# Output rows leaving in transfers of two tiles from four buffers, in a Fourier-mixing and gated feed-forward kernel

## The chip, the cores and the metric

The kernel runs on one core of a Trainium2 chip. A core has a TensorE for matrix products (PE in the profile, its weight loads PEld), a VectorE (DVE), a ScalarE (ACT), a GpSimd (POOL) and a SyncE (SP), which here only issues transfers; 16 DMA engines carry the transfers. The metric is the device time of one execution in microseconds (us), lower is better. The kernel before takes 1181.79 us in the median of three runs (1179.18, 1181.79 and 1183.06).

## The reference

The input `x` has 8 batches of 3136 rows of 256 numbers. First it is transformed by a Fourier transform over the rows and over the columns, of which the real part is kept. Then comes a gated feed-forward block:

```python
X = np.fft.fft(np.fft.fft(x, axis=1), axis=2).real          # (8, 3136, 256)
h = np.maximum(X @ w_in, 0.0)                               # (8, 3136, 1024)
conv = sum(conv_w[k] * shifted(h, k - 1) for k in range(3)) # three taps along the rows, zeros at the ends
out = (h * sigmoid(conv)) @ w_out                           # (8, 3136, 256), float32
```

`shifted(h, j)` stands for `h` moved by `j` rows.

## The kernel before

The sequence transform is done once per batch as matrix products with tables (`pd`, the `Unit`s in the code), spread over the steps of the batch before. Its results lie in `PQ`. The rest is a loop of 256 steps: 8 batches, 4 chunks of a batch, and 8 blocks of 128 columns out of the 1024 of the middle layer (`steps`, line 925). A step `(b, c, f)` goes through several engines in a software pipeline written out by hand (lines 1019 to 1052; nothing is reordered by a planner):

- `products` (line 777): two matmuls into the PSUM tiles `pb` and `pa`; `copies` (784), ScalarE, copies `pb` to `nb`; `combine` (792), VectorE, makes `h` of both, which applies the relu.
- `first_tap` (801), ScalarE, starts the tile `g` with the first tap; `middle` (806) adds the second tap by an accumulating transfer `g<-h`, which GpSimd issues; `last_tap` (810), VectorE, three steps later, adds the third.
- `sigmoid` (824), ScalarE, and `gate` (830), GpSimd and VectorE, four steps later.
- `mm2` (846), five steps later (`LAG`): TensorE multiplies each tile of 128 rows of `g` with its block of `wout` and sums over the eight blocks `f` in the PSUM tiles `po`, two row tiles in each.

The output path is the end of `mm2`. A chunk has six row tiles. The last chunk of a batch has 64 rows more; they are kept in `left`, and in an odd batch the rows left of two batches make a seventh tile. At the eighth block, when a pair of tiles in `po` is complete, ScalarE copies both to a buffer `os` in SBUF (line 861), and SP issues one transfer of 128 KB for each tile (line 863), or two of 64 KB for the seventh tile. There are three buffers `os` (line 80); a copy into a buffer waits until the transfers out of it have landed. So every eight steps there is a burst of six copies and six transfers, and at the end of the batches 1, 3, 5 and 7 one of seven copies and eight transfers.

Each engine runs its instructions strictly in the written order. Behind the copies of a burst ScalarE has the sigmoid, the copies of `pb` and of the transform's tiles (`as<-pd`, lines 381 and 405) of the next steps. SP's queue also holds the loads of `x` (`xh`, lines 119 and 126) and of a row that is spread over the partitions (`eb`, line 562).

A row of ones, `one` (line 665), lies in the pool of constants. Two matmuls before the loop read it (line 915). The pool `gp` (line 78) has seven slots that hold set-up tiles first and then the tiles `g` in turn.

Of the kernel before, what the change touches and what calls it, by code (L numbers as in the profile page):

```python
# [9 lines left out]
F32 = mybir.dt.float32  # L10
# [27 lines left out]
def kernel(  # L38
# [10 lines left out]
    nc = tc.nc  # L49
    B, S, D = x.shape  # L50
    F = moe_w_in.shape[1]
    P = 128
# [16 lines left out]
    const = ctx.enter_context(tc.tile_pool(name="const", bufs=1))  # L69
# [7 lines left out]
    hp = ctx.enter_context(tc.tile_pool(name="hp", bufs=6))  # L77
    gp = ctx.enter_context(tc.tile_pool(name="gp", bufs=7))
    nbp = ctx.enter_context(tc.tile_pool(name="nbp", bufs=2))
    osp = ctx.enter_context(tc.tile_pool(name="osp", bufs=3))  # L80
    edp = ctx.enter_context(tc.tile_pool(name="edp", bufs=1, space=DRAM))
    psa = ctx.enter_context(tc.tile_pool(name="psa", bufs=2, space=PSUM))
    psb = ctx.enter_context(tc.tile_pool(name="psb", bufs=1, space=PSUM))
# [8 lines left out]
    def mm(o, l, r, start, stop):  # L92
        nc.tensor.matmul(o, l, r, start=start, stop=stop, skip_group_check=True)  # L93
# [568 lines left out]
            for f in self.parts(c0, c1):  # L662
                f()

    one = const.tile([1, P], F32, name="one")
    nc.gpsimd.memset(one, 1.0)
    ident = gp.tile([3 * NF, 3 * NF], F32, name="ident", tag="g")
    make_identity(nc, ident)
# [87 lines left out]
    rows = out.rearrange("b s d -> (b s) d")  # L756
# [89 lines left out]
    def mm2(s):  # L846
        b, c, f = s
        ch = chunks[c]
        tiles = [(gs[s][:, o:o + m], [(0, b, r, m)]) for o, r, m in ch.tiles]
        if ch.last and b % 2:  # L850
            tiles.append((left[:, f], [(i * LEFT, b - 1 + i, ch.rest[1], LEFT) for i in range(2)]))
        for i, (w, to) in enumerate(tiles):
            if f == 0 and i % 2 == 0:
                po[b, c, i // 2] = pso.tile([P, 2, D], F32, name="po", tag="po")
            pt = po[b, c, i // 2]
            mm(pt[:, i % 2, :], w, wout[:, f, :], f == 0 and i % 2 == 0, f == NF - 1)
            if f == NF - 1 and (i % 2 or i == len(tiles) - 1):
                del po[b, c, i // 2]
                osb = osp.tile([P, 2, D], F32, name="os", tag="os")
                for j in range(i - i % 2, i + 1):  # L860
                    nc.scalar.copy(out=osb[:, j % 2], in_=pt[:, j % 2])  # L861
                    for p0, b_, r, m in tiles[j][1]:
                        nc.sync.dma_start(out=rows[b_ * S + r:b_ * S + r + m, :], in_=osb[p0:p0 + m, j % 2])
        gs.pop(s)


# [152 lines left out]
    for t in range(n + LAG):  # L1019
# [30 lines left out]
        if t >= LAG:  # L1050
            mm2(steps[t - LAG])
# [67 lines left out]
```

## Time and profile before

The profiled execution took 1182.34 us; its span, from the first instruction to the last, is 1180.6 us, and the mean granted TensorE clock 0.995.

| | us | share of the span |
|---|---|---|
| TensorE, matmuls | 1142.3 | 97% |
| TensorE, weight loads (beside the matmuls) | 889.1 | 75% |
| VectorE | 970.7 | 82% |
| ScalarE | 943.5 | 80% |
| GpSimd | 611.2 | 52% |
| copies `os<-po` on ScalarE, 196 of them | 57.8 | 5% |

The transfers `g<-h` are the largest traffic (115.83 MB on their queue); the queue of SP and ScalarE moves 50.89 MB, of which 25.7 MB are written to HBM.

In the profile a row of the timeline gives a start, a length, the engine, the line, the operation, what is written and read, and in brackets how long the engine stood idle before and who ended that. The chain of waits is the work that ended last, followed back from the end of the program. In the name of an engine a `q` means its sequencer, which waits and issues transfers. The granted clock is the share of TensorE's full clock that it was given in a stretch.

### The profile page before, as it was taken

How to read it: one execution, taken by the hardware profiler on the slowest of the kernel's cores; microseconds unless marked ns; L12 is line 12 of the kernel's file. 1: busy time of each engine (PE TensorE's matmuls, PEld its weight loads, DVE VectorE, ACT ScalarE, POOL GpSimd, SP SyncE). 2: the span in 40 equal slices, each digit the busy share in tenths (PEclk: the TensorE clock that was granted, in tenths of full speed). 3: DMA queues.
4: the chain of work that ended last, by engine and by line, in shares of the span. 5: the costliest groups of instructions: out<-in, count | busy, mean ns of one | idle time of the engine just before them, and what ended most of it. 6: DMA issues, size and time to landing. Idle time of an engine off the chain costs nothing.

```text
span 1180.6 us, 16071 instructions
## 1 busy us (share of the span) xinstructions
PE 1142.3 (97%) x4818; PEld 889.1 (75%) x4818; DVE 970.7 (82%) x1448; ACT 943.5 (80%) x1939; POOL 611.2 (52%) x734
## 2 busy tenths in 40 slices
PE   4989999999999999999998999999999999999998
PEld 2756777777777777777776777777778777777777
DVE  7589979998788789798876888888787678788885
ACT  2578878888788879888876878888887788898884
POOL 5346745666366554746464464655444344444443
PEclk9999999999999999999999999999999999999999
DMA  8767886776677676757675576865565556666664
GB/s 209 196 101 156 167 142 155 163 162 141 142 157 164 131 180 133 170 113 175 144 168 120 107 156 139 181 128 121 128 124 107 124 122 138 129 131 127 128 117 99
DMA packets 107587, 168.16 MB, mean 142 GB/s; under 512 B 32657, under 2 KB 62627, under 8 KB 107501
## 3 DMA queue, kind: packets, MB, share of 16 engines
q0 software_dynamic: 41984, 115.83, 51.3%
q1 hardware_dynamic: 64345, 50.89, 15.3%
q8 instruction: 38, 0.62, 0.2%
q10 hardware_dynamic: 1172, 0.43, 0.2%
q14 instruction: 48, 0.39, 0.1%
HBM read 38.40 MB, written 25.74 MB: 54 GB/s over the span
## 4 chain that ended last, share of the span: by engine, by line
PE 77%; ACT 5%; DVE 3%; issue 1%; DMA 1%; POOL 0%; ACTq 0%; DVEq 0%; SPq 0%
PE po L93 48%; PE pb L93 12%; PE pa L93 11%; PE pd L93 6%; ACT nb L790 1%; ACT g L828 1%; DVE g L813 1%; ACT os L861 1%; DMA out_dram<-os 1%; ACT pa L769 0%; ACT g L804 0%; DVE g L837 0%; DVE h L798 0%; DVE w L228 0%; DVE pt L418 0%
## 5 line engine op out<-in xcount | busy, mean ns | idle before, releaser
L93 PE MATMUL po<-wout,g 128*128 128x256 f32 x3072 | 709.3, 380 | 6.9 <-DVE g L837 6.2
L93 PEld LDWEIGHTS po<-wout,g 128*128 128x128 f32 x3072 | 582.7, 190 | 152.9 <-issue 20.0
L808 POOL DMA_DIRECT2D g<-h x256 | 228.3, 892 | 460.9 <-ACT g L804 247.4
L828 ACT ACTIVATE g<-g,cw 128x385 f32<-128x385 f32 (+2 forms) x512 | 291.9, 624 | 67.3 <-DVE g L813 64.8
L836 POOL TENSOR_TENSOR g<-g,h 128x385 f32<-128x385 f32 (+1 forms) x256 | 305.6, 1194 | 55.9 <-ACT g L828 54.2
L790 ACT ACTIVATE nb<-pb 128x386 f32<-128x386 f32 (+3 forms) x512 | 227.0, 498 | 113.0 <-PE pb L93 112.2
L798 DVE CUSTOM_DVE_ANT_0 h<-pa,nb 128x386 f32<-128x386 f32 (+3 forms) x512 | 264.5, 557 | 29.8 <-POOL h L775 19.8
L813 DVE SCALAR_TENSOR_TENSOR g<-h,cw,g 128x770 f32<-128x770 f32 (+1 forms) x256 | 284.1, 1110 | 0.0
L804 ACT ACTIVATE g<-h,cw 128x770 f32<-128x770 f32 (+1 forms) x256 | 244.2, 954 | 0.0
L93 PE MATMUL pb<-qt,G 127*128 127x387 f32 (+2 forms) x512 | 214.7, 500 | 2.6 <-ACT nb L790 1.1
L93 PE MATMUL pa<-pt,G 128*128 128x387 f32 (+2 forms) x512 | 213.0, 497 | 1.2 <-ACT pa L769 0.8
L837 DVE TENSOR_TENSOR g<-g,h 128x385 f32<-128x385 f32 (+1 forms) x256 | 187.3, 732 | 25.7 <-ACT g L828 25.5
L769 ACT ACTIVATE pa<-eb,ge 128x387 f32<-128x387 f32 (+2 forms) x256 | 155.1, 606 | 1.4 <-DVE h L798 1.0
L93 PEld LDWEIGHTS pa<-pt,G 128*128 128x128 f32 x512 | 96.7, 190 | 76.8 <-issue 17.3
L93 PE MATMUL pd<-tab,w 98*128 98x197 f32 (+2 forms) x448 | 98.4, 319 | 4.6 <-DVE as L412 3.8
L132 POOL DMA_INDIRECT xh<-in_x_dram,idx x64 | 91.0, 1422 | 18.3 <-issue 12.3
L93 PEld LDWEIGHTS pb<-qt,G 127*128 127x128 f32 x512 | 91.0, 191 | 9.8 <-ACT nb L790 2.9
L93 PEld LDWEIGHTS pd<-tab,w 98*128 98x128 f32 (+1 forms) x448 | 81.8, 191 | 15.0 <-ACT pa L769 5.0
L861 ACT COPY os<-po 128x256 f32<-128x256 f32 x196 | 57.8, 393 | 13.1 <-PE po L93 6.5
L168 DVE TENSOR_TENSOR xh<-xh 98x1024 f32<-98x1024 f32 (+1 forms) x32 | 46.7, 1460 | 0.1
L157 DVE TENSOR_TENSOR xh<-xh 98x1020 f32<-98x1020 f32 (+1 forms) x32 | 44.7, 1402 | 0.0
L385 DVE TENSOR_TENSOR as<-as,pd 128x196 f32<-128x196 f32 x14 | 5.0, 358 | 37.6 <-ACT as L381 37.6
(140 smaller groups left out, 449.8 us busy)
## 6 DMA issues: line engine op xcount, KB each, us to landing
g<-h POOLq DMA_DIRECT2D x192, 385.0 KB, 4.5
g<-h POOLq DMA_DIRECT2D x64, 416.0 KB, 4.5
out_dram<-os SPq DMA_DIRECT2D x192, 128.0 KB
xh<-in_x_dram SPq DMA_DIRECT2D x16, 784.0 KB
eb<-ed SPq DMA_DIRECT2D x16, 193.5 KB
raw<-in_moe_w_in_dram SPq DMA_DIRECT2D x4, 512.0 KB
raw<-in_moe_w_out_dram SPq DMA_DIRECT2D x1, 2048.0 KB
eb<-ed SPq DMA_DIRECT2D x8, 209.0 KB
```

The costliest lines, as they stand in the source:

```text
L93: nc.tensor.matmul(o, l, r, start=start, stop=stop, skip_group_check=True)
L132: nc.gpsimd.indirect_dma_start(out=xh[b, h][0:NP, 7 - m].rearrange("p q d -> p (q d)"), out_offset=None, in_=bass.AP(tensor=x.tensor, offs ...
L769: act(pa[s][:, 0:n], eb[b, c], AF.Copy, scale=ge[:, f:f + 1])
L790: act(nb[s][:, i, cols], p[:, cols], AF.Copy, scale=-1.0 if i else 1.0)
L798: nc.vector._custom_dve(TENSOR_ADD_SAT, out=to, in0=a[:, cols], in1=c[:, i, cols], s0=BIG, s1=0.0)
L804: act(gs[s], hs[s][:, 0:n], AF.Copy, scale=cw[:, 0, s[2]:s[2] + 1])
L808: nc.gpsimd.dma_start(out=gs[s], in_=hs[s][:, 1:1 + n], accum_op=ALU.add)
L813: stt(out=g, in0=h[:, k:k + n], scalar=cw[:, k, f:f + 1], in1=g, op0=ALU.mult, op1=ALU.add)
L828: act(gs[s][:, c], gs[s][:, c], AF.Sigmoid, scale=cw[:, 1, s[2]:s[2] + 1])
L836: gt(g[:, p], g[:, p], h[:, p], op=ALU.mult)
L837: vt(g[:, v], g[:, v], h[:, v], op=ALU.mult)
L861: nc.scalar.copy(out=osb[:, j % 2], in_=pt[:, j % 2])
```

## The change

The buffers `os` become four. When a pair of tiles is complete, both are copied, and then one transfer of 256 KB takes both to their two places in the output, each with 128 rows of 1 KB. The single seventh tile goes as before. The row `one` moves from the constants to a slot of `gp`.

```diff
-    osp = ctx.enter_context(tc.tile_pool(name="osp", bufs=3))
+    osp = ctx.enter_context(tc.tile_pool(name="osp", bufs=4))
...
-    one = const.tile([1, P], F32, name="one")
+    one = gp.tile([1, P], F32, name="one", tag="g")
     nc.gpsimd.memset(one, 1.0)
...
                 osb = osp.tile([P, 2, D], F32, name="os", tag="os")
                 for j in range(i - i % 2, i + 1):
                     nc.scalar.copy(out=osb[:, j % 2], in_=pt[:, j % 2])
-                    for p0, b_, r, m in tiles[j][1]:
-                        nc.sync.dma_start(out=rows[b_ * S + r:b_ * S + r + m, :], in_=osb[p0:p0 + m, j % 2])
+                if i % 2:
+                    r0, r1 = (tiles[j][1][0][2] for j in (i - 1, i))
+                    nc.sync.dma_start(out=bass.AP(
+                        tensor=out.tensor, offset=out.offset + (b * S + r0) * D,
+                        ap=[[D, P], [(r1 - r0) * D, 2], [1, D]]), in_=osb)
+                else:
+                    for p0, b_, r, m in tiles[i][1]:
+                        nc.sync.dma_start(out=rows[b_ * S + r:b_ * S + r + m, :], in_=osb[p0:p0 + m, 0])
```

## The prediction

> **What bounds the kernel now.** I read the page's busy times first, then the list of what the output buffer `os` waits for, then the timeline around those waits, the chain of waits, and the granted clock in those stretches.
>
> ```profile
> PE 1142.3 (97%) x4818; PEld 889.1 (75%) x4818; DVE 970.7 (82%) x1448; ACT 943.5 (80%) x1939; POOL 611.2 (52%) x734
> ...
> L861 ACT COPY os<-po 128x256 f32<-128x256 f32 x196 | 57.8, 393 | 13.1 <-PE po L93 6.5
> ...
> g<-h POOLq DMA_DIRECT2D x192, 385.0 KB, 4.5
> ...
> out_dram<-os SPq DMA_DIRECT2D x192, 128.0 KB
> xh<-in_x_dram SPq DMA_DIRECT2D x16, 784.0 KB
> ```
>
> TensorE is busy for 97% of the span, and its matmuls are the same before and after. So only two things can change the time: moments at which TensorE stands still, and the tail behind its last matmul. The list for the tile `os` shows what the output path does to the other engines:
>
> ```profile
> L863 SPq DMA_DIRECT2D out_dram<-os x200: 332/404/2663, 106.7 to 1177.3; - x100
> L861 ACT COPY os<-po x196: 345/394/441, 106.3 to 1176.3; 128x256 f32<-128x256 f32 x196
>   DMA out_dram<-os: 5.5, 3
> ```
>
> Of 200 transfers only three landings are seen to be awaited, for 5.5 us in all; everything else about them is hidden. All the waits sit in one place. A chunk ends with three pairs of tiles, which fit three buffers; the last chunk of an odd batch has a seventh tile, and its copy needs a fourth buffer. The timeline of ScalarE (start, length, work, and in brackets its idle time before and who ended it) shows that copy in batches 1, 3, 5 and 7, and the six copies that run before it in batch 3:
>
> ```profile
> 361.11 0.37 ACT L861 COPY os<-po 128x256 f32<-128x256 f32 x1 [1.03 <-PE pa L93]
> ...
> 635.80 1.74 ACT L861 COPY os<-po 128x256 f32<-128x256 f32 x6
> ...
> 641.73 0.37 ACT L861 COPY os<-po 128x256 f32<-128x256 f32 x1 [4.19 <-DMA out_dram<-os]
> ...
> 920.96 0.37 ACT L861 COPY os<-po 128x256 f32<-128x256 f32 x1 [0.98 <-DMA out_dram<-os]
> ...
> 1176.27 0.37 ACT L861 COPY os<-po 128x256 f32<-128x256 f32 x1 [0.35 <-DMA out_dram<-os]
> ```
>
> The reader is to see 1.03, 4.19, 0.98 and 0.35 us in which ScalarE stands behind a landing (the first is put down to TensorE, but it is the same place at the same distance from the first transfer). The chain of waits, its TensorE pieces compared, says what TensorE lost:
>
> ```profile
> 356.65 3.02 PE po L93 x14
> 360.97 2.59 PE po L93 x12
> 364.88 2.59 PE po L93 x12
> ...
> 629.43 3.02 PE po L93 x14
> ...
> 636.62 4.96 DMA out_dram<-os
> ...
> 648.25 3.69 PE po L93 x12
> ...
> 653.47 2.59 PE po L93 x12
> ...
> 911.87 3.02 PE po L93 x14
> ...
> 919.06 1.80 DMA out_dram<-os
> ...
> 926.52 2.86 PE po L93 x12
> ...
> 930.91 2.59 PE po L93 x12
> ```
>
> In batch 1 the steps go on at 4.32 and 3.91 us, with no loss. The stretch from the seventh step of the last chunk to the second step of the next batch takes 653.47 - 629.43 = 24.04 us in batch 3 and 930.91 - 911.87 = 19.04 us in batch 5, for the same matmuls: batch 3 loses 5.00 us more. TensorE's own rows show the stops, and the windows the granted clock (third number from the right, PEclk):
>
> ```profile
> 638.62 2.75 PE L93 MATMUL po<-wout,g 128*128 128x256 f32 x12
> 644.90 0.72 PE L93 MATMUL pd<-tab,w 99*128 99x99 f32 x2 [3.53 <-DVE as L412]
> ...
> 921.07 2.75 PE L93 MATMUL po<-wout,g 128*128 128x256 f32 x12
> 924.13 0.44 PE L93 MATMUL pd<-tab,w 99*128 99x99 f32 x2 [0.31 <-DVE as L412]
> ...
> 926.52 2.86 PE L93 MATMUL po<-wout,g 128*128 128x256 f32 x12 [0.63 <-DVE g L837]
> ```
>
> ```profile
> 640.00:645.00 5.00, 1.47 (x8) 1.00 (x6) 0.84 (x3) 3.27 (x8) 0.90 (x2) 0.85 0.44 140
> 645.00:649.00 4.00, 4.00 (x9) 2.60 (x10) 4.00 (x7) 2.63 (x7) 1.78 (x3) 0.50 0.50 96
> ...
> 921.00:925.00 4.00, 3.69 (x17) 2.80 (x16) 1.61 (x5) 3.67 (x8) 0.94 (x3) 1.00 0.88 229
> ```
>
> Batch 5 loses 0.31 + 0.63 = 0.94 us and keeps its clock at 1.00. Batch 3 loses 5.00 + 0.94 = 5.94 us: 3.53 us of standstill, and about 2.4 us because the clock is then granted at 0.50.
>
> **The change part by part.**
>
> *Fourth buffer.* The seventh tile no longer needs a buffer of its own chunk: with four it takes the one last used by the preceding chunk, eight steps (over 30 us) earlier. The three waits go, and batch 1's. What is late next: at batch 3 everything behind the copy on ScalarE moves 4.19 us forward, so the matmul that waited until 644.90 could start at 640.71, and TensorE is free at 638.62 + 2.75 = 641.37. At batch 5 the two waits would end at 923.15 and 925.54; TensorE is free at 923.82 and, by the lengths of its rows, at 925.89. So neither stop survives, with 0.35 us in hand at the tighter. Gain 5.94 + 0.94 + 0 (batch 1) = 6.9 us; a leftover of up to 0.4 us at batch 3 is possible, and the gain is at least the 3.53 + 0.94 of plain standstill.
>
> *One transfer for two.* 96 pairs leave by one issue instead of two; the eight half tiles of the odd batches leave as before. SP's rows:
>
> ```profile
> 364.28 0.38 SPq L119 DMA_DIRECT2D xh<-in_x_dram  x1
> ...
> 636.62 1.71 SPq L863 DMA_DIRECT2D out_dram<-os  x1
> ...
> 919.06 0.38 SPq L863 DMA_DIRECT2D out_dram<-os  x1
> ...
> 1173.95 3.99 SPq L863 DMA_DIRECT2D out_dram<-os  x8
> 1177.35 0.59 SPq L863 DMA_DIRECT2D out_dram<-os  x1
> ```
>
> An issue of 784 KB costs SP 0.38 us, as one of 128 KB does, so I take 0.4 us for one of 256 KB and drop 96 x 0.4 = 38 us of SP's time. None of that is on the path: what stands behind these issues on SP are loads of `eb` and `xh`, which are wanted whole steps later. The first half of a pair leaves later by one copy (1.74 / 6 = 0.29 us); nobody waits for it once the buffers suffice. The bytes and the pieces of 1 KB are the same. ScalarE's and TensorE's instructions are unchanged, and ScalarE has one landing to look at per buffer, not two.
>
> *The row of ones* moves into a slot of `g`. It is read by two matmuls at 41.9 us, before the loop; the slot is next written by the third `first_tap`, after these. Cost nothing.
>
> *Tail.* The last copy starts 0.35 us earlier, and SP is free for its two halves after three issues, not six. That takes about 0.4 us off the end. The last three whole issues hold the same bytes, so I bound this at -0.6 (a larger transfer lands later) and +1.0.
>
> Sum: 5.9 + 0.9 + 0.4 = 7.2 us, of the profiled execution's 1182.34: 1175.1, or a span of 1173.4. The median of the runs shown, 1181.79, is 0.55 us under the profiled one, so 1175 stands for both.
>
> A rule to weigh: the Trainium skill, "DMA: Bandwidth & Descriptors", section "Anatomy of one DMA", gives a transfer a fixed cost of about 2.0 us whatever its size. By that, as an estimate, 96 transfers fewer would save 192 us if they were on the path; the trace has four landings awaited out of 200, so here the rule decides nothing but those.
>
> **The rivals.**
>
> *The long wait is an accident (A).* For: three of the four landings come soon (1.80 us behind the issue in batch 5), and in batch 3 alone the second issue took 1.71 us where 0.38 is usual. If the usual execution has a batch 3 like batch 5, only 0.94 + 0.94 + 0.4 = 2.3 us can be gained: 1181.79 - 2.3 = 1179.5. Against: the median run is as long as the profiled one, which holds the 5.94; the fastest, 1179.18, may be one without it. What makes such a wait dear is the clock. The Trainium skill, "TensorE: Matmul & The Clock Gate", Part 1, halves the clock after an idle window of some 3.4 us; the rows agree, 0.50 after 3.53 us and 1.00 after 0.31. By that rule a landing a few tenths sooner in batch 3 would already spare 2.4 us, and the gain would be about 4.8: 1177.0.
>
> *Pair transfers hold up the accumulating ones (B), slower.* Three transfers of 256 KB stand in the engines' rings at once, ahead of or beside the transfer `g<-h` of that step, where today six of 128 KB trickle in over some 4 us.
>
> ```profile
> L808 POOL DMA_DIRECT2D g<-h x120: 865/878/976, 645.7 to 1148.0; - x120
> DMA to landing us min/median/max: 3.9/4.6/7.1
> ...
> L813 DVE SCALAR_TENSOR_TENSOR g<-h,cw,g 128x770 f32<-128x770 f32 x192 | 205.1, 1068 | 0.0
> ```
>
> Its reader, `last_tap`, comes three steps later, some 3 x 4.2 = 12.6 us, and has no idle time today; the slowest landing is 7.1 us. At the tail 832 KB of output take about 5 us from first issue to landing, so 768 KB would add at most 4.6: 4.6 + 4.6 = 9.2 us, or 11.7 from the slowest. It decides from 12.6 us; each microsecond beyond would cost the 32 chunk ends 32 us less the 7.2, and half a microsecond gives 1175 + 16 = 1191. The Trainium skill, the same DMA page, section "Queues, rings and completion order", says the engines take turns between queues packet by packet, which would let a bigger backlog slow the other queue; no row here shows by how much.
>
> *The merged form does not help and something else waits (C):* for example a load behind SP's longer hold of the copies; nothing in the rows speaks for it, and it would leave about 1181.
>
> **How the numbers follow.** My forecast (both stops gone) 0.64, at 1175.1, own range 1173 to 1177.5; A 0.19, at 1177 to 1179.5; B 0.12, at 1185 to 1191; C 0.05. The runs shown spread from 2.6 under to 1.3 over their median. The range goes from 1175.1 - 2.6 = 1172.5 up through A and C to 1181.8, which leaves out B and a little more. 0.3% is 3.5 us, about what a measurement can tell from no change: faster means under 1178.2. Faster 0.64 + a third of A = 0.70, same 0.17, slower 0.13.
>
> **What would show it.** Right: the seventh copy of batches 1, 3, 5 and 7 follows the sixth with no wait for a landing; the stretch that took 24.04 us takes about 18.1, and the one of 19.04 about 18.1; the clock stays at 1.00 there; SP has 104 output issues of about 0.4 us; the last issue starts about 0.4 us sooner behind the last matmul. Wrong: idle time of `last_tap` (B), landings of `g<-h` beyond 12 us (B), another wait in those stretches (C), or the median of the kernel before, in new runs, with a batch 3 that loses no more than batch 5 (A).

## The result and the profile after

| | median (us) | lowest to highest | runs |
|---|---|---|---|
| before | 1181.06 | 1177.18 to 1184.51 | 9 |
| after | 1175.36 | 1172.81 to 1176.11 | 9 |

The ratio of after to before is 0.9955, with a 95% interval of 0.9939 to 0.9970: by the ratio the changed kernel is faster by 5.3 us, 3.5 to 7.2; the two medians differ by 5.7. The span of its profiled execution is 1173.4 us, where the prediction's sum gave 1173.4.

The page's busy times, and the list for the tile `os`, of the kernel after:

```profile
span 1173.4 us, 15901 instructions
PE 1139.6 (97%) x4818; PEld 887.5 (76%) x4818; DVE 970.7 (83%) x1448; ACT 942.9 (80%) x1939; POOL 606.9 (52%) x734
```

```profile
L861 ACT COPY os<-po x196: 350/395/442, 106.4 to 1169.0; 128x256 f32<-128x256 f32 x196
L864 SPq DMA_DIRECT2D out_dram<-os x96: 372/373/2722, 107.0 to 1169.2; - x96
L869 SPq DMA_DIRECT2D out_dram<-os x8: 478/1055/1349, 361.0 to 1170.2; - x8
its engine sat idle before it (us, times) until:
  PE po L93: 6.5, 3
```

The same work is done by the same instructions on TensorE (4818 matmuls); the landing of the output is gone from the list of what the copies wait for. An issue of 256 KB has a median of 0.373 us. ScalarE's timeline shows the seven copies of batches 1, 3 and 5 now in one row each, and in batch 7 the seventh right behind the sixth:

```profile
358.82 2.02 ACT L861 COPY os<-po 128x256 f32<-128x256 f32 x7
636.24 2.01 ACT L861 COPY os<-po 128x256 f32<-128x256 f32 x7
912.57 2.01 ACT L861 COPY os<-po 128x256 f32<-128x256 f32 x7
1168.51 0.93 ACT L861 COPY os<-po 128x256 f32<-128x256 f32 x3 [0.22 <-PE po L93]
```

The chain of waits of after, for the two stretches that the prediction measured, and the windows around the places of the former stops (PEclk is the third number from the right):

```profile
629.87 3.02 PE po L93 x14
643.45 2.86 PE po L93 x12
647.83 2.59 PE po L93 x12
...
906.20 3.02 PE po L93 x14
919.77 2.86 PE po L93 x12
924.15 2.59 PE po L93 x12
```

```profile
635.00:640.00 5.00, 5.00 (x23) 4.04 (x23) 1.52 (x4) 5.00 (x15) 1.78 (x3) 1.00 0.56 124
640.00:645.00 5.00, 4.90 (x22) 3.65 (x21) 4.68 (x9) 3.63 (x9) 1.78 (x3) 1.00 0.90 223
645.00:650.00 5.00, 5.00 (x24) 4.04 (x23) 5.00 (x8) 5.00 (x10) 1.78 (x2) 1.00 0.36 67
...
915.00:920.00 5.00, 4.90 (x21) 3.50 (x20) 3.36 (x7) 3.64 (x9) 1.79 (x4) 1.00 0.91 221
```

Batch 3's stretch takes 647.83 - 629.87 = 17.96 us instead of 24.04, batch 5's 924.15 - 906.20 = 17.95 instead of 19.04. The granted clock stays at 1.00. TensorE is busy for 4.90 of 5.00 us in one window of each stretch: a stop of 0.10 us is left in front of the matmuls that start at 643.45 and 919.77.

The first full step of the last chunk in batches 3, 5 and 7 serves as a mark, so that the gain can be divided among the parts of the execution. Chain of waits of before, then of after:

```profile
601.35 3.02 PE po L93 x14
...
883.79 3.02 PE po L93 x14
...
1150.09 3.02 PE po L93 x14
```

```profile
601.79 3.02 PE po L93 x14
...
878.12 3.02 PE po L93 x14
...
1143.32 3.02 PE po L93 x14
```

| part of the execution | after less before (us) |
|---|---|
| to batch 3's mark | +0.44 |
| to batch 5's mark (end of batch 3 in it) | -6.11 |
| to batch 7's mark (end of batch 5 in it) | -1.10 |
| to the end (tail in it) | -0.43 |
| span | -7.2 |

### The profile page after: what moved, and what is told of

The parts are those of the page before. It is cut to its first block, busy times and chain, and to the rows that moved or that the text cites. A ratio compares the mean times of both kernels' runs of the same rounds, so it can differ in the third digit from the quotient of the medians.

```text
span 1173.4 us, 15901 instructions
## 1 busy us (share of the span) xinstructions
PE 1139.6 (97%) x4818; PEld 887.5 (76%) x4818; DVE 970.7 (83%) x1448; ACT 942.9 (80%) x1939; POOL 606.9 (52%) x734
## 4 chain that ended last, share of the span: by engine, by line
PE 77%; ACT 4%; DVE 3%; issue 1%; DMA 0%; POOL 0%; ACTq 0%; DVEq 0%
PE po L93 49%; PE pb L93 12%; PE pa L93 11%; PE pd L93 6%; ACT nb L790 1%; DVE g L813 1%; ACT os L861 1%; ACT g L828 1%; DMA out_dram<-os 0%; ACT pa L769 0%; DVE g L837 0%; DVE w L228 0%; DVE xh L168 0%; ACT g L804 0%; DVE pt L418 0%
## 5 line engine op out<-in xcount | busy, mean ns | idle before, releaser
L836 POOL TENSOR_TENSOR g<-g,h 128x385 f32<-128x385 f32 (+1 forms) x256 | 301.2, 1177 | 49.5 <-ACT g L828 47.9
```

The lines of the kernel that those rows point to most:

```text
L836: gt(g[:, p], g[:, p], h[:, p], op=ALU.mult)
```

## Experiments

Each kernel differs from the kernel before, or from the changed one, as its diff shows. Where a fourth or an extra buffer is added, or the set-up row is named, the row `one` lies in a slot of `gp`, as in the change.

**Four buffers alone**

```diff
-    osp = ctx.enter_context(tc.tile_pool(name="osp", bufs=3))
+    osp = ctx.enter_context(tc.tile_pool(name="osp", bufs=4))
...
-    one = const.tile([1, P], F32, name="one")
+    one = gp.tile([1, P], F32, name="one", tag="g")
```

> Four buffers, one transfer per tile as in the kernel before, the row of ones in a slot of g. Theory 1 (the buffer is the cause): the seventh copies of batches 1, 3, 5 and 7 follow the sixth with no wait, TensorE has no stop at the ends of batches 3 and 5, and 6.9 of the 7.2 us of the prediction come; only the tail keeps its eight issues, so 0.4 us less gain than the changed kernel: some 6 us under the kernel before in the median. Theory 2 (the transfer of two tiles is the cause): at most 1 us.

Measured: 1175.31 us (1174.16 to 1177.56), ratio to before 0.9945 (0.9929 to 0.9961); span 1173.2. The list for `os`, with 200 issues as before:

```profile
L863 SPq DMA_DIRECT2D out_dram<-os x200: 332/404/2492, 106.7 to 1170.0; - x100
...
  PE po L93: 6.5, 3
```

No landing is awaited, and the time is that of the whole change. The fourth buffer is the cause; merging the transfers isn't needed for it. The 0.4 us that the merged form should have kept at the tail can't be told apart in the medians (1175.31 and 1175.36). In the profiled executions it is there: the span ends 4.85 us behind the last matmul in this run, 4.50 in the changed kernel and 4.93 in the kernel before.

**Transfers of two tiles alone**

```diff
 (against the kernel after)
-    osp = ctx.enter_context(tc.tile_pool(name="osp", bufs=4))
+    osp = ctx.enter_context(tc.tile_pool(name="osp", bufs=3))
```

> Transfers of two tiles from three buffers, the row of ones in a slot of g. The seventh copy has to wait for the landing of the chunk's first pair, which is issued about 0.3 us later than the first tile is in the kernel before. Theory 1a: landings stay as they were, so a wait of 1 to 1.5 us in batches 1 and 5 and of about 4 us in batch 3; no gain beyond the tail's 0.4 us. Theory 1b: in batch 3 it was the second issue of the burst that was held up (1.71 us instead of 0.38), and the pair leaves whole with the first issue, so that its landing comes after some 2 us: the wait in batch 3 falls to 1 to 1.5 us, TensorE keeps its clock, and 4 to 5 of the 7.2 us come without a fourth buffer. Theory 2 (the merged transfer alone is the cause): all 7 us.

Measured: 1178.50 us (1177.24 to 1180.60), ratio 0.9973 (0.9963 to 0.9983). ScalarE's rows for the seventh copies of batches 3 and 5, and TensorE's stops behind them:

```profile
640.19 0.37 ACT L861 COPY os<-po 128x256 f32<-128x256 f32 x1 [1.20 <-DMA out_dram<-os]
...
917.80 0.37 ACT L861 COPY os<-po 128x256 f32<-128x256 f32 x1 [1.26 <-PE pa L93]
```

```profile
643.36 0.44 PE L93 MATMUL pd<-tab,w 99*128 99x99 f32 x2 [0.53 <-DVE as L412]
645.75 1.56 PE L93 MATMUL po<-wout,g 128*128 128x256 f32 x6 [0.63 <-DVE g L837]
...
920.97 0.44 PE L93 MATMUL pd<-tab,w 99*128 99x99 f32 x2 [0.58 <-DVE as L412]
923.36 1.99 PE L93 MATMUL po<-wout,g 128*128 128x256 f32 x8 [0.63 <-DVE g L837]
```

The windows around batch 3's copy and behind it keep their granted clock of 1.00:

```profile
639.00:644.00 5.00, 4.47 (x20) 3.19 (x19) 1.38 (x4) 3.70 (x8) 0.90 (x2) 1.00 0.98 251
644.00:649.00 5.00, 4.37 (x20) 3.17 (x19) 5.00 (x8) 3.75 (x8) 1.78 (x3) 1.00 0.44 82
```

It went as theory 1b said: the wait of batch 3 is 1.20 us, the slow clock stays away, and the merged form alone gains some 2.9 us in the medians (1181.37 to 1178.50; 2.0 to 4.4 by the ratio's interval), less than the 4 to 5 expected. It keeps stops of 0.53 + 0.63 = 1.16 and 0.58 + 0.63 = 1.21 us, which the fourth buffer takes down to 0.10. The reason that the theory gave isn't tested here: in this run no issue of batch 3's burst was held up at all (0.38, 0.37 and 0.37 us).

**A buffer more in batch 3 alone**

```diff
     osp = ctx.enter_context(tc.tile_pool(name="osp", bufs=3))
+    osx = ctx.enter_context(tc.tile_pool(name="osx", bufs=1))
...
-                osb = osp.tile([P, 2, D], F32, name="os", tag="os")
+                osb = (osx if b == 3 and i % 2 == 0 else osp).tile([P, 2, D], F32, name="os", tag="os")
```

> The kernel before with one buffer more that only the seventh tile of batch 3 uses. Theory 1: the stop of batch 3 goes and the others stay, so the stretch of 24.04 us falls to about 18.1 and that of batch 5 stays near 19.0; the median falls by 5 to 6 us. Theory A (the long wait of batch 3 is an accident of the profiled execution): the median falls by 1 us or so.

Measured: 1175.94 us (1175.07 to 1178.18), ratio 0.9955 (0.9939 to 0.9971): 5.4 us under the kernel before in the medians. Its chain of waits (the lines are one further down):

```profile
628.32 3.02 PE po L94 x14
...
646.28 2.59 PE po L94 x12
...
904.65 3.02 PE po L94 x14
...
923.67 2.59 PE po L94 x12
```

Batch 3's stretch is 17.96 us, batch 5's still 19.02. One wait in one batch is most of the gain, in the median too (3.4 to 7.2 us by the ratio's interval); theory A, an accident of the profiled execution worth 1 us or so, falls.

**The row of ones alone**

```diff
-    one = const.tile([1, P], F32, name="one")
+    one = gp.tile([1, P], F32, name="one", tag="g")
```

> The kernel before with only the row of ones moved to a slot of g: all theories expect no difference, within 1 us of the kernel before, and the same waits of the seventh copies. A gain here would mean that the new places of the tiles in memory matter.

Measured: 1180.76 us (1179.04 to 1184.43), ratio 0.9999 (0.9985 to 1.0012). No difference, as expected. Its profile holds the stop of batch 3 again, in ScalarE's row and in the windows:

```profile
642.16 0.37 ACT L861 COPY os<-po 128x256 f32<-128x256 f32 x1 [4.69 <-DMA out_dram<-os]
```

```profile
640.00:645.00 5.00, 1.32 (x7) 0.81 (x5) 0.44 (x2) 2.84 (x8) 0.90 (x2) 1.00 0.44 137
645.00:649.00 4.00, 3.67 (x9) 2.42 (x10) 3.96 (x8) 2.64 (x7) 1.78 (x3) 0.57 0.40 76
```

The clock falls to 0.57 behind the stop. So two profiled executions of three-buffer kernels with single transfers show the same long wait at the same place. Why just there?

**Why batch 3: TensorE's code fetched at another time**

The trace has a record of every DMA packet; the engines' instructions, too, are fetched by such packets, in a queue of their own (called code here). I summed the packets by their start in steps of 0.5 us from the first issue of a burst; KB of output queue, of the accumulating queue, and of code:

```
before, batch 3, from 636.2 us    output  0 46  75  2   0  5  7 157   accumulating 0 0 21 90  90 93 75  9   code 16 in the first 0.5 us
before, batch 5, from 918.6 us    output  0 47 133 76   1  4  5  81   accumulating 0 0  0 63  99 93 93 36   code  0
ones alone, batch 3, from 636.1   output  0 45  75  3   0  0 12 159   accumulating 0 0 21 93  90 90 69  9   code 16 in the first 0.5 us
```

While the accumulating transfer `g<-h` runs, the output queue gets next to nothing: 0 to 7 KB in 0.5 us against 75 to 99. In batch 5 it starts 1.69 us behind the burst's first issue, just as the first two output transfers (256 KB) come to their end (1.87 us). In batch 3, 16 KB of code start to arrive 0.48 us behind the first issue, SP's second issue takes 1.71 us, the accumulating transfer starts 1.46 us behind the first issue, 0.23 us sooner than in batch 5, and the second output transfer comes only when it is done.

The other bursts of these traces fit that. In the kernel before, the second issue of a burst takes 0.33 to 0.38 us in 30 of the 32 bursts. The other two are batch 3's and one at 428.0 us (1.26 us), and they are the two in which a 16 KB block starts to arrive within the first 0.5 us. With the row of ones alone, the block at the burst of 427.94 us comes 0.71 us behind the first issue, and there the third issue takes 1.87 us. In these two earlier bursts no copy needs a buffer of its own burst. In the last one the accumulating transfer starts 1.69 us behind its own issue, where 1.65 to 1.70 are usual in that run: an issue is held up there although the accumulating transfer does not start sooner.

To test this I shifted the code: the six idle matmuls of the set-up are cut into 24 smaller ones.

```diff
-    keep_on([idle] * 6)
+    for _ in range(6):
+        for s_ in range(2):
+            for q_ in range(2):
+                mm(idle.rearrange("p (s q d) -> p s q d", s=2, q=2)[:, s_, q_], wt[0][1][0:NP, 1, 0],
+                   wt[0][1][0:NP, s_, q_], True, True)
```

> The kernel before, with the six idle 512-column matmuls of the set-up cut into 24 of 128 columns: as much work for the array and 72 instructions more on TensorE, so that every later block of TensorE's code is fetched some two steps earlier. Theory F (a 16 KB block of TensorE's code that arrives with the first issue of batch 3's burst makes the accumulating transfer overtake and holds the second issue): the second issue of that burst takes 0.4 us, the landing comes after 1.8 us, the seventh copy waits about 1.0 us, TensorE loses about 1 us there and keeps its clock, and the median falls by about 5 us with three buffers and single transfers. Theory G (something else at that place, such as the transfers of the transform's rows): the second issue still takes over 1.2 us, the wait stays over 3.5 us, and the median stays within 1 us.

Measured: 1177.19 us (1175.95 to 1179.67), ratio 0.9968 (0.9954 to 0.9982). Fetches of 16 KB, which in the kernel before came in the microseconds 605, 636 and 671, came in 595, 625 and 657; those of 8 KB stayed within some us of their places (before 610, 643, 646; here 609, 639, 641). So the 16 KB blocks are TensorE's. SP's second issue in batch 3, the seventh copy, the chain's landing and TensorE's stops in this run:

```profile
635.40 0.38 SPq L863 DMA_DIRECT2D out_dram<-os  x1
```

```profile
637.37 0.37 ACT L861 COPY os<-po 128x256 f32<-128x256 f32 x1 [1.05 <-DMA out_dram<-os]
```

```profile
635.40 1.81 DMA out_dram<-os
```

```profile
640.54 0.44 PE L93 MATMUL pd<-tab,w 99*128 99x99 f32 x2 [0.38 <-DVE as L412]
642.93 2.86 PE L93 MATMUL po<-wout,g 128*128 128x256 f32 x12 [0.63 <-DVE g L837]
```

The packets from 635.0 us are much like those of batch 5: output 0, 47, 132, 77, 0, 3, 7, 82 KB, accumulating 0, 0, 0, 63, 102, 93, 90, 36, code 0. The issue takes 0.38 us instead of 1.71, the landing 1.81 instead of 4.96, and the kernel with three buffers and single transfers gains 3.7 us in the medians (1180.84 to 1177.19; 2.1 to 5.4 by the ratio's interval), a little less than expected. Theory F holds as to what sets off the long wait: the block of code that arrives with the burst. By what path the fetch holds up the issue, these runs don't show.

**The same shift in the changed kernel.** The diff is the one above, against the kernel after.

> The changed kernel with the same 72 instructions. Nobody waits there for a landing any more, so both theories expect the changed kernel's time within 1 us, 1175.4; a fall below it would mean that the shifted code saves something elsewhere, and that the gain of the run before this one isn't that of batch 3.

Measured: 1175.18 us (1172.82 to 1175.29), ratio to before 0.9952 (0.9934 to 0.9970), as the changed kernel. The shift is worth nothing where no landing is awaited. In the changed kernel itself, where the block starts to arrive 0.08 us ahead of the burst's first issue, the second issue of batch 3 is still held up, and nobody minds:

```profile
636.91 0.38 SPq L864 DMA_DIRECT2D out_dram<-os  x1
637.46 1.27 SPq L864 DMA_DIRECT2D out_dram<-os  x1
```

The accumulating transfer starts 1.89 us behind its own issue there and 1.90 in batch 5, so here, too, its start is not what holds up the issue. The first 256 KB of output are through 2.77 us behind the first issue, against 1.82 in batch 5 of this kernel and 3.93 in batch 3 of the kernel before: with the fetch at about the same place, the merged form softens the delay and does not remove it. In the run of merged transfers from three buffers, the block had started to arrive 0.85 us ahead of the first issue; that run escaped it.

**Two buffers.** The diff is that of the four buffers, with `bufs=2`.

> The kernel before with two buffers: the third pair of every chunk end waits for the landing of the first, about 0.4 + 0.4 + 1.8 us behind the first copy, so some 1.5 us in each of 32 chunk ends. If such a wait costs TensorE all of it: 48 us more. If TensorE has slack there as in batch 1 (1.03 us awaited, nothing lost): 10 us or less more. From batch 5 (0.98 us awaited, 0.94 lost) I expect between these, 10 to 45 us more.

Measured: 1231.97 us (1228.48 to 1234.55), ratio 1.0434 (1.0402 to 1.0465): 51 us more. The list for `os` and the page:

```profile
  DMA out_dram<-os: 74.3, 34
```

```profile
PE 1155.8 (94%) x4818; PEld 892.6 (73%) x4818; DVE 969.3 (79%) x1448; ACT 943.1 (77%) x1939; POOL 594.2 (48%) x734
```

The waits are longer than I expected, 74.3 / 34 = 2.2 us each instead of 1.5, and the loss, 51 / 74.3, is some 0.7 of what ScalarE waits. I had expected 10 to 45 us of 48, a share of 0.2 to 0.9, so it was the wait that was taken too low; the share lies inside.

**The very last half tile by another queue** (against the kernel after)

```diff
                     for p0, b_, r, m in tiles[i][1]:
-                        nc.sync.dma_start(out=rows[b_ * S + r:b_ * S + r + m, :], in_=osb[p0:p0 + m, 0])
+                        eng = nc.scalar if b == B - 1 and p0 else nc.sync
+                        eng.dma_start(out=rows[b_ * S + r:b_ * S + r + m, :], in_=osb[p0:p0 + m, 0])
```

> The changed kernel, the second half of the very last tile issued by ScalarE instead of SP. The last issue then does not stand behind four others and starts about 0.5 us sooner; up to 0.6 us off the tail behind the last matmul, which the median can hardly show. If the tail is set by the landing of the data and not by the issues: no difference, also not in the profile.

Measured: 1174.84 us (1172.96 to 1177.04), ratio to before 0.9955 (0.9940 to 0.9969). ScalarE's row of the last copies in this run:

```profile
1167.96 0.93 ACT L861 COPY os<-po 128x256 f32<-128x256 f32 x3 [0.22 <-PE po L93]
```

From the start of that row to the end of the span are 1172.5 - 1167.96 = 4.54 us, in the changed kernel 1173.4 - 1168.51 = 4.89. Some 0.35 us are there in the profile, but the medians (1174.84 and 1175.36) can't tell them from nothing, so no version is shown to beat the changed kernel.

## Why the prediction was right

*Fourth buffer.* The mechanism and its two places were right: no wait at any of the four copies, stretches of 17.96 and 17.95 us where 18.1 was said, clock at 1.00. Between the marks, the end of batch 3 gave 6.11 us (5.94 said) and that of batch 5 1.10 (0.94 said). The four-buffer run shows that this step alone makes the whole measured gain. One reading was wrong without harm: the 0.35 us in hand at batch 5. The 925.89 at which TensorE is free there still contains the first stop of 0.31; without it TensorE is free at 925.58, and the wait ends at 925.54, which leaves 0.04. In the profile after, the second stop is not gone but some 0.1 us long, in both batches.

*One transfer for two.* An issue of 256 KB takes 0.37 us (0.4 said), and in the presence of the fourth buffer the merging moves nothing that the medians show. The prediction put it at nothing but the tail, which is right for the change as made. It did not say that with three buffers the merging alone would gain 2.9 us. How much of that is due to the awaited pair leaving with the burst's first issue, and how much to the fetch missing the burst in that kernel, isn't shown. The fixed cost of about 2.0 us that the prediction weighs is given by the Trainium skill, "DMA: Bandwidth & Descriptors", section "Anatomy of one DMA", for transfers that GpSimd issues, and these are issued by SP. In the kernel before, the awaited landings in the chain came 1.80 us behind the issue in batches 5 and 7, and 4.96 in batch 3, where the issue was held up.

*Tail.* 0.43 us between the last mark and the end, 0.4 said.

*The row of ones.* Ratio 0.9999; nothing, as said.

*The size against the median.* The sum of 7.2 us is that of the two profiled executions. In the medians the gain is 5.7 us, with 7.2 at the very end of the interval. Two pairs of runs bear on the term of batch 3, 5.94 us in the profiled execution: the buffer for batch 3 alone gains 5.4 us (3.4 to 7.2), and the shifted code gains 3.7 (2.1 to 5.4) and leaves 0.38 + 0.63 = 1.0 us of that stop, so 4.7. Both medians lie lower than 5.94, but the intervals hold it. So it isn't shown whether this term is smaller in the usual execution, or whether the profiled execution of before was long for another reason. Rival A in its full form, a gain of 2.3 us, fell.

*Luck.* That 1175.1 was said and 1175.36 came is in part luck: the sum was taken off the profiled 1182.34, which is 1.3 us above the new median of before, and the sum was 1.5 us larger than the gain in the medians; the two nearly cancel. That the span came out at 1173.4 to the tenth is luck, too: the three terms gave 0.36 us more than was said, and up to batch 3's mark 0.44 us were lost for which the prediction has no term.

*Rival B* fell: the accumulating transfers landed nowhere near the 12.6 us at which it decides. The list of their issues from 640 to 1150 us in the kernel after:

```profile
L808 POOL DMA_DIRECT2D g<-h x122: 862/876/981, 641.9 to 1149.6; - x122
DMA to landing us min/median/max: 3.9/4.1/6.8
```

The median is 4.1 us and the longest 6.8. The 4.6 of before is no measure for the change: the run with the row of ones alone has 4.1, too, and the four-buffer run with single transfers 4.1 and 7.3. At the chunk ends themselves the packets show a small delay of the kind that rival B feared: the accumulating transfer starts 1.91 us behind its issue in the median (1.67 before, 1.45 away from the bursts), and its last packet ends 4.46 us behind it (4.28 before). Once it runs, it is the output that gives way. The Trainium skill, "DMA: Bandwidth & Descriptors", section "Queues, rings and completion order", has the engines take turns between queues packet by packet and gives no shares in bytes; here the accumulating queue got 90 KB or more for each few KB of the output queue, and the merged form of the output cost it some 0.2 us. (The tail holds 896 KB, not the 832 of the prediction, so that rival B's bound would be 4.4 us and not 4.6; nothing hung on that.)

*Rival C* did not show: after the change no wait of the output path is left in those stretches.

## What to carry to other kernels

When the busiest engine is at 97%, look for the few places where another engine's wait reaches it, and count buffers against the largest burst, not the usual one: here four pairs met three buffers in four of 32 chunk ends. Price a wait by what the busy engine loses, slow clock included, and not by the wait: 1.03 us cost nothing, 0.98 cost 0.94, 4.19 cost about 6. A long wait at a single place that comes back in another execution, as this one did, can be due to where the code happens to be fetched. A buffer that takes the wait away makes the kernel safe from that; shifting the code moves the fetch elsewhere.

## What the hardware showed that was not expected

- A 16 KB block of TensorE's code that arrives at the first issue of a burst goes with a held-up issue on SP (1.71 us instead of 0.38) and brought an output transfer's landing to 4.96 us, where 1.80 was seen in batch 5; with the code shifted it was 1.81. A block that started to arrive 0.85 us ahead of the first issue held up none.
- While an accumulating transfer of some 400 KB ran, about 2 us, SP's output queue moved 0 to 7 KB in 0.5 us.
- An issue on SP took as long for 256 KB (0.37 us) as for 128 KB (0.38) or 784 KB (0.38), unless it was held up, at such a fetch or while the accumulating transfer ran (1.2 us and more).
